# A spectral block's gradients on one core: c's gradient as a row, tables in two parts, one block placed elsewhere, more buffers at the end, another order

## The chip, the core and the metric

The kernel runs on one core of a Trainium2 chip. The core has five engines that run side by side, each with its own queue of instructions in a fixed order: PE (TensorE, matrix products; PEld is its loading of weights), DVE (VectorE), ACT (ScalarE), POOL (GpSimd) and SP (SyncE, which here does nothing but issue transfers). Sixteen DMA engines move data between DRAM and the on-chip memory SBUF; matrix products land in PSUM. Waits between engines go by semaphores. The metric is device time in microseconds (us) of one execution.

## What is computed

Forward and backward of one block, with x of 2048 rows by 512, in bfloat16. The reference is the vjp of this function, and returns its output and nine gradients:

```python
def _A_ref(x, w_r, w_i):                       # a filter in the 2-D Fourier domain
    X = rfft2(x) * (w_r + 1j * w_i)            # 2048 x 257 coefficients
    return irfft2(X, (S, D))
def _B_ref(x, w1, b1, w2, b2):                 # 512 -> 1792 -> 512
    r = relu(x @ w1 + b1); h = r * r
    return h @ w2 + b2
mod = (silu(c) @ w_mod)                        # six rows of 512: sa, ca, ga, sb, cb, gb
h = layernorm(x) * (1 + ca) + sa
x = x + ga * _A_ref(h, A_w_r, A_w_i)
h = layernorm(x) * (1 + cb) + sb
return x + gb * _B_ref(h, B_w1, B_b1, B_w2, B_b2)
```

The outputs are out_0 (the block's output) and the gradients of A_x (out_1), A_w_r and A_w_i (out_2, out_3), B_w1, B_b1, B_w2, B_b2 (out_4 to out_7), c (out_8, 512 values) and w_mod (out_9).

## The kernel before

The Fourier transforms are matrix products with tables of sines that are made on the chip. The rows' transform goes in two steps, with the table TA and with the tables LF; LF has 16 blocks of 128 by 128, each in three parts (first, second, and the first negated), so that real and imaginary parts come out of plain products. LG is LF transposed, for the way back. Cd and Cf are the tables of the columns' transform. The negated part lets a product read parts 0, 1 or 1, 2 as neighbours.

The work runs in stages:

- **Start (0 to about 50 us)**: loads, tables (`build_lf` makes LF on DVE and ACT), the modulation rows, the layer norm of 16 row tiles, and the first transform step (`spec_f1_half`). Between them PE makes products of grad_out with w2 transposed (`back_products`, L837), which nothing else waits for yet.
- **First spectrum (about 50 to 85 us)**: `spec_f23` makes the coefficients Xs in eight groups; `cmul` (L415 to L418, DVE) multiplies them with the filter Z; every second group Xs is stored to the scratch tensor xs_dram (L869). Beside it `lg_part` transposes a quarter of LF into LG by a DMA (L850) and stores it to LG_dram (L852); L826 stores LF to LF_dram. `spec_g1` (L352, L355) goes back with LG.
- **Four row blocks (about 85 to 265 us)**: `stage_g`, `stage_h` (L1009), `stage_o` and `stage_gn` (both L1038): the second layer norm, the dense part, its backward, and the transform of the gradient.
- **Second spectrum (about 265 to 330 us)**: `spec_f23` on the gradient, with LF reloaded in four pieces LFb (L1170, L1311), the filter Z and the stored Xs reloaded into two blocks Xb (L1314, buffers Xb_0 and Xb_1). `cmul` makes the filter's gradients in place in Xb, which L1332, L1337 and L1339 store to out_2 and out_3. Between its groups PE fills in `grad_w1` (L1281). LG comes back as LGb (L1346), and `spec_g1` uses it. L1359 loads grad_out again as g_sb in two halves, which `scale_g` (L1400) multiplies.
- **Last stage (about 330 us to the end)**: pairs of rows go through `spec_g2` (L372, its result Tsb is written by ACT at L374), `spec_g3` (L382), and `row_pair` and `row_end` (L1448 to L1468) to out_1. PE fills in the rest of `grad_w1` and then `grad_w2` (L1378), one of 14 blocks hn against g_sb at a time; hn is loaded from h_dram by a DMA transpose (L1201). `gm.emit` (L459 to L473) makes w_mod's gradient and sums for c, and L1498 to L1502 finish c's gradient.

At the very end c's gradient stands as gcb, 128 partitions by 4 values, and is stored with each value to its own place:

```python
with nc.allow_non_contiguous_dma(reason="512 values"):
    nc.sync.dma_start(out_8.rearrange("b (dc p) -> p (b dc)", p=P), gcb)
```

Memory is handed out by pools that are stacked, some from the left and some from the right (`Slots`). A tile in a pool that lies where a released pool was has to wait until the last reader of the old tile is done, a store among them. Before the change the stack on the left is, from below: gw1 and G (`gwa`), the LGb tables (`lg2`), Z (`spb`), then Xb and the products p (`f23b`, `ewb`); the buffers of the last stage (`fin2`, called fp) come from the right over the place of the upper ones.

The order of the instructions is written out by hand: `ORDER` has a list per engine. The numbers count that engine's instructions in the order in which the program makes them (SP: its 290 DMA issues); `set_order` ties each to the one before it in the list. So an SP issue that waits holds up all issues behind it.

Of the kernel before, what the change touches and what calls it, by code (L numbers as in the profile page):

```python
# [198 lines left out]
def build_lf(tc, K, cpool, g, sm, krs):  # L199
# [23 lines left out]
    LF = cpool.tile([P, 16, 3, P], BF16, name="LF")  # L223
    K["LF"] = [LF[:, 2 * gi:2 * gi + 2] for gi in range(8)]
    K["LFall"] = LF
    for q in range(4):
# [10 lines left out]
        for i in range(2):  # L237
            for x in range(2):
                V.tensor_tensor(LF[:, 4 * q + n0:4 * q + 4, i, 64 * x:64 * x + 64].rearrange("p n (a b) -> p n a b", b=4),
                                w[:, i, n0:4, 64 * x:64 * x + 64].rearrange("p n (a b) -> p n a b", b=4),  # L240
                                mk[:, x, None, None, :].broadcast_to([P, 4 - n0, 16, 4]), op=ALU.mult)
            for h in range(n0):
                V.tensor_tensor(LF[:, h, i, 0:64].rearrange("p (a b) -> p a b", b=4), w[:, i, h, 0:64].rearrange("p (a b) -> p a b", b=4),
                                mk[:, 2 + h, None, :].broadcast_to([P, 16, 4]), op=ALU.mult)
                V.tensor_tensor(LF[:, h, i, 64:128].rearrange("p (j a b) -> p j a b", j=2, b=2),
                                w[:, i, h, 64:128].rearrange("p (j a b) -> p j a b", j=2, b=2),
                                mk[:, 4, :].rearrange("p (j b) -> p j b", j=2)[:, :, None, :].broadcast_to([P, 2, 16, 2]), op=ALU.mult)
        nc.scalar.activation(LF[:, 4 * q:4 * q + 4, 2, :], LF[:, 4 * q:4 * q + 4, 0, :], AF.Copy, scale=-1.0)

# [56 lines left out]
def spec_f23(tc, K, UT, AEs, dc, dest, elementwise, after=lambda gi: None):  # L306

    nc = tc.nc
    with Slots(tc, name="psB", bufs=1, space=PSUM) as psB_pool, \
         Slots(tc, name="psC", bufs=2, space=PSUM) as psC_pool:  # L310
        def f3(gi):
            ae = AEs[gi % 2]
            tl = dest(gi)
            for hh in range(2):
                ps = psC_pool.tile([P, 2, 512], FP32, name="psC")
                for o in range(2):
                    for cs in range(2):
                        nc.tensor.matmul(ps[:, o, 0:DF], lhsT=K["LF"][gi][:, hh, o + cs, :], rhs=ae[:, hh, 256 * cs:256 * cs + DF],
                                         start=(cs == 0), stop=(cs == 1))
# [22 lines left out]
def spec_g1(tc, K, Z, CS, after=None):  # L342

    nc = tc.nc
    with Slots(tc, name="psG", bufs=6, space=PSUM) as psG_pool:
        for gi in range(8):
            for hh in range(2):
                n = 2 * gi + hh
                ps = psG_pool.tile([P, 2, 2 * P], FP32, name="psG")
                for y in range(2):  # L350
                    for ri in range(2):
                        nc.tensor.matmul(ps[:, 0, P * y:P * y + P], lhsT=Z[gi][:, hh, ri, 2 * y:255 + 2 * y:2],  # L352
                                         rhs=K["LG"][:, n, ri + y, :], start=(ri == 0), stop=(ri == 1))
                for ri in range(2):
                    nc.tensor.matmul(ps[:, 1, :], lhsT=Z[gi][:, hh, ri, 1:256:2],  # L355
                                     rhs=K["LG"][:, n, ri:ri + 2, :].rearrange("p y m -> p (y m)"), start=(ri == 0), stop=(ri == 1))
# [84 lines left out]
class GMod:  # L441
# [12 lines left out]
    def emit(self, jc, q, row, pool, ppool, nbuf=2, last=False):  # L454
# [24 lines left out]
        "0-17 106 18-21 135-142 22-27 143-146 28-29 147-154 30-31 155-158 32-35 159-166 36-37 167-170 38-45 175-178 171-174 50-51 "  # L479
        "183-186 179-182 52-53 86-89 46-47 187-190 48-49 191-194 90-93 195-202 58-61 54-57 203-206 94-97 66-69 211-214 98-101 "  # L480
        "62-65 207-210 102-105 70-71 107-110 74-75 72-73 76-77 219-222 215-218 78-85 111-126 223-226 303 127-134 304-311 227-234 "
        "312-321 235-242 328-330 243-246 322-323 331-334 324-325 335 326-327 251-254 336-337 340-343 338-339 247-250 344-359 "
        "255-258 360-366 372-373 367 374-375 368-369 259-262 370-371 376-383 388-389 263-266 390-391 384-385 448-451 386-387 "
        "452-455 460-463 456-459 267-270 464-470 476-477 471 478-479 472-475 271-274 484-487 480-483 279-282 275-278 512-513 "
        "488-489 514-517 287-290 490-491 500-501 283-286 518-519 492-493 506-507 494-495 502-503 496-497 504-505 508-509 498-499 "
        "510-511 548-549 520-521 524-525 550-551 526-527 522-523 528-529 536-537 530-535 538-539 542-543 540-541 544-545 552-555 "
        "546-547 560-563 566-569 556-559 564-565 578-579 572-573 570-571 580-581 574-577 582-583 291-294 585-588 295-298 589-593 "
        "299-302 594-598 392-395 608-611 607 396-399 612 653-656 400-403 666-669 665 404-407 679-682 678 408-411 692 412-415 693 "
        "691 416-419 599 420-423 600 694 601-603 695 604-606 424-427 849-852 428-435 696 862-864 436-439 865 613 440-443 614-620 "
        "444-447 861 883-885 584 621-624 641-644 625-632 886 633-640 645-652 657-664 670-677 683-690 697-808 896-897 809-824 898 "  # L490
        "825-832 841-848 853-860 899 866-869 833-840 874-881 870-873 882 887-895 901-914 900 1053 915-928 1054 929-942 1055-1056 "
        "943-956 1066 957-970 1067 971-1012 1068 1017-1020 1013-1016 1021-1024 1029-1032 1025-1028 1069 1065 1033-1036 1045-1052 "
        "1057-1064 1070-1073 1087-1090 1037-1044 1078-1085 1074-1077 1086 1091-1094 1100 1099 1101-1102 1095-1098 1103 1105-1118 "
        "1104 1119-1232 1253 1249 1233-1236 1250 1254-1255 1237-1248 1251 1257-1264 1252 1256 1269-1272 1265-1268 1281-1284 "
        "1305-1311 1285-1296 1301-1304 1297-1300 1273 1277-1278 1274 1327-1333 1279 1316-1322 1280 1338-1344 1323-1325 1275-1276 "
        "1349-1355 1312-1315 1326 1360-1366 1371-1377 1334 1382-1388 1345 1335 1346 1336 1347 1337 1348 1393-1406 1367-1370 "
        "1356-1359 1407-1420 1378-1379 1389-1390 1380 1391 1381 1392 1437-1450 1425-1427 1421 1428 1422-1424 1451-1464 1433 "
        "1429-1430 1434 1431 1435-1436 1432 1465-1488 1505-1520 1489-1491 1521 1497-1498 1492 1501-1502 1493 1503-1504 1494 "
        "1499-1500 1495-1496 1538-1553 1522-1524 1530-1531 1534-1535 1532-1533 1525-1528 1536-1537 1529 1554-1633 1643-1644 "
        "1635-1638 1647-1648 1645-1646 1639-1641 1649-1650 1642 1651-1666 1683 1691-1692 1695-1698 1634 1684-1689 1693-1694 "  # L500
        "1699-1714 1690 1667-1682 1744-1745 1732-1733 1731 1734-1735 1746-1747 1736-1738 1740-1743 1739 1715-1730 1764-1779 "
        "1748-1763 1781-1782 1793-1794 1789-1790 1795-1796 1780 1791-1792 1783-1788 1797-1812 1829-1830 1837-1838 1831-1832 "
        "1839-1844 1833-1836 1813-1828 1865-1866 1861-1862 1867-1868 1863-1864 1845-1860 1891-1892 1909-1910 1885-1886 1915-1916 "
        "1887-1888 1893-1894 1917-1918 1911-1912 1895-1896 1919-1920 1903-1906 1897-1902 1913-1914 1889-1890 1907-1908 1869-1884 "
        "1927-1930 1951-1954 1921-1922 1933-1934 1931-1932 1939-1940 1923-1926 1941-1942 1945-1946 1943-1944 1935-1938 1947-1948 "
        "1963-1966 1957-1958 1967-1968 1955-1956 1975-1976 1959-1960 1969-1970 1961-1962 1977-1978 1971-1972 1979-1980 1973-1974 "
        "1949-1950 1989-2004 1981-1988 2005 2007-2012 2006 2013-2030 2053 2048 2054 2049 2055 2050 2056 2051-2052 2047 2031-2046 "
        "2079 2083 2073 2084 2080-2081 2074 2082 2085-2086 2057-2072 2129 2125 2130 2119 2126-2127 2209-2224 2075-2078 2121-2124 "
        "2128 2131-2132 2087-2102 2155 2120 2156 2103-2118 2133-2148 2159-2160 2150 2161-2162 2157-2158 2149 2163-2178 2201-2202 "
        "2205-2208 2203 2196 2204 2179-2194 2151-2154 2197-2200 2243-2246 2309-2310 2195 2225-2240 2251 2247 2252-2254 2248 2242 "  # L510
        "2249-2250 2255-2270 2241 2277-2292 2272 2271 2293-2308 2311-2326 2273-2276 2327-2416"
    ),
    "ACT": (
        "0-1 3 2 8 7 4-6 13 10 16 50 11 51 17 12 9 52-53 20 14 54 15 55 18-19 56 23-24 57 37-38 58 27 21-22 42 59-60 30 26 25 31 "
        "39 29 34 40 28 62 61 44 32 41 33 63 45 35 43 36 46 64 79 47 65 80 66 48 67 81-83 68 84-86 88 87 69 89 91 90 92 49 94 93 "
        "104 106 105 70 107 109 108 77 71 110-111 73 72 78 112-114 74 115-119 121 75 122-124 128 76 132 131 95 133 147 96 151 150 "
        "158 125 154 97 126 98 127 161 99 162 129 100 134 187 130 135 101 136 102 191 163 137 103 138 120 139-146 148-149 152-153 "
        "159-160 155 164 157 156 166 198 167 165 168-170 173 171-172 174 179 176 180-181 175 182-183 178 184-186 177 188-190 192 "
        "202 194 193 199 201 200 203 195 197 196 227 204-210 212 211 213-214 220 215 219 216 221-223 218 224-226 217 231 228-229 "
        "238 230 232 234 233 239-243 235 237 236 244 247 245-246 248-250 252 251 254 253 259-260 255 261-262 256 264 263 267-268 "  # L520
# [1028 lines left out]
```

## Time and profile before

| | us |
|---|---|
| three runs: median (lowest to highest) | 424.77 (424.04 to 427.11) |
| the profiled execution, whole | 424.7 |
| its span | 422.9 |
| PE busy in the span | 382.3 (2417 matmuls) |
| DVE, ACT busy | 342.7, 276.7 |
| DMA | 93.59 MB, 221 GB/s on average |
| last matmul ends | 405.65 |
| mean granted clock of TensorE | 0.974 of full |

The profile is of one execution. Its times count from the start of the span. A row of the timeline has start, duration, engine, line, operation, the tile written and the tiles read, and in brackets the idle time before it and what ended it. A row of the waits has who waited, for what, and in total, how often and the longest. A row by stretches has the stretch, its length, the busy time of PE, PEld, DVE, ACT and POOL (with the count of instructions), the granted clock as a share, the mean busy share of the DMA engines, and GB/s. In the page's second part the span is cut in 40 equal slices, and each digit is a busy share in tenths. "To landing" is the time from a DMA's issue until its semaphore says that it has landed.

### The profile page before, as it was taken

Reading aid. Unit: us, or ns where it says so; the run is one execution under the profiler, and the core shown is the slowest. Engines: PE = TensorE matmul, PEld = TensorE weight load, DVE = VectorE, ACT = ScalarE, POOL = GpSimd, SP = SyncE. Lnnn points to the kernel's source line nnn. Section 1 sums busy time; section 2 is a strip of 40 time slices with the busy share of each in tenths; the row PEclk is TensorE's granted clock in tenths of the full one; section 3 lists DMA queues with packets and bytes.
Section 4 is the critical chain, followed back from the end, with each engine's and each line's share of the span. In section 5 each row is a group of like instructions: output and inputs, shape, how many; then the busy total and the mean of one; then the engine's idle time right before and its main releaser. Section 6 shows DMA issues by size and latency. Waiting matters only on the chain.

```text
span 422.9 us, 6929 instructions
## 1 busy us (share of the span) xinstructions
PE 382.3 (90%) x2417; PEld 201.3 (48%) x2417; DVE 342.7 (81%) x826; ACT 276.7 (65%) x493; POOL 14.4 (3%) x56
## 2 busy tenths in 40 slices
PE   0799999989999999999999999999999499999930
PEld 0355565745444444444444454655567354444430
DVE  6899879956996999799999999289999177877930
ACT  4569999779733793487168584676564378678920
POOL 5322000000000000000000000000000000000000
PEclk9999999999999999999999999999999799999975
DMA  8999999998855595669659989899899999999750
GB/s 256 212 251 285 288 208 255 298 201 239 285 110 173 146 244 133 133 182 222 173 130 233 244 222 262 241 351 342 236 324 213 228 187 255 267 242 233 195 155 0
DMA packets 144212, 93.59 MB, mean 221 GB/s; under 512 B 98347, under 2 KB 130097, under 8 KB 143665
## 3 DMA queue, kind: packets, MB, share of 16 engines
q1 hardware_dynamic: 143468, 92.55, 87.0%
q10 hardware_dynamic: 708, 0.59, 0.6%
q8 instruction: 19, 0.31, 0.3%
q14 instruction: 17, 0.13, 0.1%
HBM read 37.39 MB, written 34.24 MB: 169 GB/s over the span
## 4 chain that ended last, share of the span: by engine, by line
PE 62%; DVE 11%; DMA 9%; SPq 8%; ACT 4%; issue 2%; ACTq 0%; DVEq 0%
PE og_0s L1038 9%; PE og_1s L1038 9%; PE mm_0s L1281 5%; PE mm_1s L1378 5%; PE mm_1s L1009 4%; PE mm_0s L1009 4%; PE mm_1s L837 3%; PE mm_1s L1281 3%; PE mm_0s L1378 3%; PE mm_0s L837 3%; PE pst L1009 3%; DMA xs_dram<-Xs_3s 2%; SPq L692 2%; SPq L689 2%; DMA g_sb<-in_grad_out_dram 2%
## 5 line engine op out<-in xcount | busy, mean ns | idle before, releaser
L1281 PEld LDWEIGHTS <-h_sb 128*128 128x128 bf16 x256 | 25.0, 99 | 22.5 <-issue 1.8
L1038 PEld LDWEIGHTS <-gab 128*128 128x128 bf16 x224 | 21.6, 98 | 25.5 <-DVE gab L1016 0.7
L1009 PEld LDWEIGHTS <-w 128*128 128x128 bf16 x224 | 21.2, 98 | 25.1 <-issue 1.9
L837 PEld LDWEIGHTS <-w2T 128*128 128x128 bf16 x224 | 21.4, 99 | 21.7 <-DMA w2T<-in_B_w_dram 2.9
L1281 PE MATMUL mm_0s<-gab,h_sb 128*128 128x384 bf16 (+1 forms) x160 | 30.2, 342 | 0.0
L1038 PE MATMUL og_0s<-w1T,gab 128*128 128x512 bf16 x112 | 26.0, 379 | 0.0
L1038 PE MATMUL og_1s<-w1T,gab 128*128 128x512 bf16 x112 | 25.7, 379 | 0.0
L336 ACT ACTIVATE AE<-psB 128x1024 bf16<-128x1024 f32 x16 | 22.0, 1375 | 1.6 <-PE psB L332 1.4
L1281 PE MATMUL mm_1s<-gab,h_sb 128*128 128x512 bf16 (+1 forms) x96 | 21.9, 384 | 0.0
L1009 PE MATMUL mm_1s<-h2T,w 128*128 128x512 bf16 x84 | 21.6, 379 | 0.0
L1009 PE MATMUL mm_0s<-h2T,w 128*128 128x512 bf16 x80 | 20.5, 379 | 0.0
L1378 PE MATMUL mm_1s<-g_sb,hn_0s 128*128 128x512 bf16 x80 | 18.1, 379 | 1.3 <-ACT gw_0s L1379 1.0
L1378 PE MATMUL mm_0s<-g_sb,hn_1s 128*128 128x512 bf16 (+1 forms) x80 | 16.4, 358 | 0.0
L837 PE MATMUL mm_1s<-gT_0s,w2T 128*128 128x512 bf16 x56 | 14.4, 379 | 1.9 <-DMA w2T<-in_B_w_dram 1.9
L837 PE MATMUL mm_0s<-gT_0s,w2T 128*128 128x512 bf16 x56 | 15.2, 395 | 0.5 <-DMA w2T<-in_B_w_dram 0.5
L372 PEld LDWEIGHTS <-utcs 128*128 128x128 bf16 x128 | 10.6, 100 | 10.3 <-issue 3.8
L1009 PE MATMUL pst<-h2T,w 128*128 128x512 bf16 x60 | 15.4, 379 | 0.0
L837 PE MATMUL mm_0s<-gT_1s,w2T 128*128 128x512 bf16 x56 | 14.4, 379 | 0.0
L837 PE MATMUL mm_1s<-gT_1s,w2T 128*128 128x512 bf16 x56 | 14.4, 378 | 0.0
L841 ACT CAST gab<-mm_1s 128x512 bf16<-128x512 f32 x20 | 12.0, 601 | 3.1 <-PE mm_1s L837 3.0
L1378 PEld LDWEIGHTS <-hn_1s 128*128 128x128 bf16 x96 | 9.3, 98 | 7.6
L1378 PEld LDWEIGHTS <-hn_0s 128*128 128x128 bf16 x80 | 7.7, 97 | 10.6 <-issue 1.9
(622 smaller groups left out, 1031.2 us busy)
## 6 DMA issues: line engine op xcount, KB each, us to landing
w<-in_B_w_dram SPq DMA_DIRECT2D x2, 1792.0 KB
Z<-wz_dram SPq DMA_DIRECT2D x4, 514.0 KB, 5.3
x_sb<-in_A_x_dram SPq DMA_DIRECT2D x2, 1024.0 KB, 7.3
n_dram<-x_sb SPq DMA_DIRECT2D x4, 512.0 KB, 3.2
h_dram<-h2r SPq DMA_DIRECT2D x8, 256.0 KB, 2.3
h_sb<-h_dram SPq DMA_DIRECT2D x4, 512.0 KB
g_sb<-in_grad_out_dram SPq DMA_DIRECT2D x2, 1024.0 KB
LF_dram<-LF SPq DMA_DIRECT2D x4, 384.0 KB, 5.8
```

The costliest lines, as they stand in the source:

```text
L336: nc.scalar.activation(dst, ps.rearrange("p r (s e f) -> p (r s) e f", s=2, e=2), AF.Copy, scale=EF_S)
L372: nc.tensor.matmul(ps[:, P * i:P * i + P], lhsT=CS[:, t, i].rearrange("p a b -> p (a b)"), rhs=K["Cf"][:, i, :], start=True, stop=True)
L689: q.dma_start(w2T[:, :, a:z], B_w2[a:z, :], transpose=True)
L692: q.dma_start(gT[b].rearrange("p j c q -> p (j c) q"), g_view[:, TB * b:TB * b + TB, :].rearrange("p j d -> p (j d)"), transpose=True)
L837: nc.tensor.matmul(ps, lhsT=w2T[:, dc, fc * P:(fc + 1) * P], rhs=gT[b][:, :, dc, :], start=(dc == 0), stop=(dc == 3))
L841: nc.scalar.copy(out=gaT[b][:, fc, :], in_=ps)
L1009: nc.tensor.matmul(ps, lhsT=w1[:, dc, (fc + i) * P:(fc + i + 1) * P], rhs=h2T[b][:, :, dc, :], start=(dc == 0), stop=(dc == 3))
L1038: nc.tensor.matmul(ps, lhsT=lhs(fc), rhs=rhs[:, fc, :], start=(fc == 0), stop=(fc == NFC - 1))
L1281: nc.tensor.matmul(blocks(ps, fb), lhsT=h2_sb[:, t, dc * P:(dc + 1) * P], rhs=gh_rows(t, fb), start=(t == 0), stop=(t == NT - 1))
L1378: nc.tensor.matmul(ps[:, 0:w], lhsT=hns[fc][:, t, :], rhs=g_sb[:, t, c:c + w], start=(t == 0), stop=(t == NT - 1))
```

## The change

c's gradient gcb is transposed on PE into PSUM (4 rows of 128), copied to SBUF by DVE, and stored as four rows of 256 bytes.

The tables LF and LG are laid out anew: by quarters, then by part, then by block. Their scratch tensors LF_dram and LG_dram hold two parts instead of three; stores, transposes and reloads move two parts, and the third is made on the chip: LG's by DVE behind each transpose, LFb's and LGb's by ACT behind each reload.

Of the two blocks Xb the second gets a pool of its own, `frb`, below the tables in the stack; it is released after the load of rows 4.

The pool at the end (`endp`) has six hn buffers instead of four, and once it exists also eight gw buffers, gh1 and q1 (three each) and gs (six); before that these have two each. hn is loaded up to ten blocks ahead instead of eight.

All five lists of `ORDER` are new.

```diff
-    LF = cpool.tile([P, 16, 3, P], BF16, name="LF")
-    K["LF"] = [LF[:, 2 * gi:2 * gi + 2] for gi in range(8)]
+    LF = cpool.tile([P, 4, 3, 4, P], BF16, name="LF")
+    K["LF"] = [LF[:, gi // 2, :, 2 * (gi % 2):2 * (gi % 2) + 2] for gi in range(8)]
...
-                                     rhs=K["LG"][:, n, ri:ri + 2, :].rearrange("p y m -> p (y m)"), start=(ri == 0), stop=(ri == 1))
+                    nc.tensor.matmul(ps[:, 1, :].rearrange("p (y m) -> p y m", y=2), lhsT=Z[gi][:, hh, ri, 1:256:2],
+                                     rhs=K["LG"][:, n // 4, ri:ri + 2, n % 4, :], start=(ri == 0), stop=(ri == 1))
...
-        "2249-2250 2255-2270 2241 2277-2292 2272 2271 2293-2308 2311-2326 2273-2276 2327-2416"
+        "2225-2240 2271 2255-2270 2272 2277-2308 2273-2276 2327-2334 2309-2326 2351 2335-2350 2368 2352-2367 2369-2417"
...
-        "2 4 0-1 7 3 18 5 8 10 22 6 9 11 30 26 15 21 29 19 116 16 49 12 20 14 17 87 27 23 31 91 28 79 34 25 35 43 24 41 13 38 37 "
+        "2 4 0-1 7 10 3 5-6 8 118 23 9 29 19 11 28 30 14 16 12 20 15 17 26 21 49 31 116 25 32 38 22 18 27 24 41 122 79 13 35 46 "
...
-        "200 208 215 217 201 225 214 209 219 193 220 202 223 221 232 227-228 230 229 231 222 226 235 213 234 224 233 236 247 253 "
-        "266 246 238 267 245 242 240 252 239 251 243-244 258 254 249-250 248 237 264 269 262 256 255 241 272 263 259-260 274 257 "
-        "268 261 276-277 271 273 279 275 281 265 280 278 282 284 270 283 285 287 286 289 288"
+        "216 211 181 179 199 203 213 225 218 201 220 198 219 212 182 184 214 224 222 221 229 236 227 237 228 226 233 232 231 230 "
+        "241 234 247 235 246 253 267-268 239 251-252 260 245 243 255 240 242 272 244 249 274 264 256 258 257 269 262 276 259 250 "
+        "254 263 271 275 238 261 279 277-278 270 265-266 248 283 282 284 280 285 287 281 286 288 273 289"
...
-    LF_dram = dram.tile([4, P, 4, 3, P], BF16, name="LF_dram")
-    LG_dram = dram.tile([4, P, 4, 3, P], BF16, name="LG_dram")
+    LF_dram = dram.tile([4, P, 2, 4, P], BF16, name="LF_dram")
+    LG_dram = dram.tile([4, P, 2, 4, P], BF16, name="LG_dram")
...
     def lg_part(q):
-        nc.sync.dma_start(K["LG"][:, 4 * q:4 * q + 4].rearrange("p a y m -> p (a y) m"),
-                          K["LFall"][:, 4 * q:4 * q + 4].rearrange("p a y m -> p (a y m)"), transpose=True)
-        nc.sync.dma_start(LG_dram[q], K["LG"][:, 4 * q:4 * q + 4])
+        nc.sync.dma_start(K["LG"][:, q, 0:2].rearrange("p y a m -> p (y a) m"), K["LFall"][:, q, 0:2].rearrange("p y a m -> p (y a m)"), transpose=True)
+        nc.vector.tensor_scalar(K["LG"][:, q, 2], K["LG"][:, q, 0], -1.0, None, op0=ALU.mult)
+        nc.sync.dma_start(LG_dram[q], K["LG"][:, q, 0:2])
...
-                    nc.sync.dma_start(LF1[g], LF_dram[g])
+                    nc.sync.dma_start(LF1[g][:, 0:2], LF_dram[g])
+                    nc.scalar.activation(LF1[g][:, 2], LF1[g][:, 0], AF.Copy, scale=-1.0)
...
-            hns.append(pool.tile([P, NT, P], BF16, name="hn", bufs=2 if pool is not endp.get("hn") else 4))
+            hns.append(pool.tile([P, NT, P], BF16, name="hn", bufs=2 if pool is not endp.get("hn") else 6))
...
     gwa = Slots(tc, name="gwa", bufs=1)
+    frb = Slots(tc, name="frb", bufs=1)
     lg2 = Slots(tc, name="lg2", bufs=1)
...
-                nc.sync.dma_start(LF2[g - 2], LF_dram[g])
+                nc.sync.dma_start(LF2[g - 2][:, 0:2], LF_dram[g])
+                nc.scalar.activation(LF2[g - 2][:, 2], LF2[g - 2][:, 0], AF.Copy, scale=-1.0)
...
-                Xt[0] = fr.tile([P, 2, 2, 4, FP], BF16, name="Xb", bufs=2)
+                Xt[0] = (frb if g else fr).tile([P, 2, 2, 4, FP], BF16, name="Xb", bufs=1)
...
-                    nc.sync.dma_start(K["LG"][:, 4 * k:4 * k + 4], LG_dram[k])
+                    nc.sync.dma_start(K["LG"][:, k, 0:2], LG_dram[k])
+                    nc.scalar.activation(K["LG"][:, k, 2], K["LG"][:, k, 0], AF.Copy, scale=-1.0)
...
-            last = fc == NFC - 1
-            gwh[fc] = (endp["gm"] if last else gwp).tile([P, D], BF16, name="gw", bufs=1 if last else 3)
+            late_ = "gm" in endp
+            gwh[fc] = (endp["gm"] if late_ else gwp).tile([P, D], BF16, name="gw", bufs=8 if late_ else 2)
...
-        while len(hns) < min(NFC, max(fc + 4, min(2 * fc + 6, 8))):
+        while len(hns) < min(NFC, max(fc + 4, min(2 * fc + 6, 10))):
...
     load_rows3(4)
+    frb.release()
...
-            gh1 = fp.tile([P, 2, D], BF16, name="gh1", bufs=3)
-            q1 = fp.tile([P, 2, D], BF16, name="q1", bufs=3)
+            gh1, q1 = [(endp["gm"].tile([P, 2, D], BF16, name=x, bufs=3) if "gm" in endp else fp.tile([P, 2, D], BF16, name=x, bufs=2)) for x in ("gh1", "q1")]
             gn = fp.tile([P, 2, D], BF16, name="gn")
-            gs = fp.tile([P, 2, D], BF16, name="gs", bufs=3)
+            gs = (endp["gm"].tile([P, 2, D], BF16, name="gs", bufs=6) if "gm" in endp else fp.tile([P, 2, D], BF16, name="gs", bufs=2))
...
-        with nc.allow_non_contiguous_dma(reason="512 values"):
-            nc.sync.dma_start(out_8.rearrange("b (dc p) -> p (b dc)", p=P), gcb)
+        pg = psX.tile([4, P], BF16, name="mm")
+        nc.tensor.transpose(pg, gcb, K["ident"])
+        gcr = fp.tile([4, P], BF16, name="gcr", bufs=1)
+        nc.vector.tensor_copy(gcr, pg)
+        nc.sync.dma_start(out_8.rearrange("b (dc p) -> (b dc) p", p=P), gcr)
```

## The prediction

> **What bounds the kernel now.** I read four views in this order: the page's first two parts, the waits, the timeline around the two longest gaps, and busy time by stretches. The first shows that TensorE sets the pace, and that the last fortieth of the span has nothing on any engine.
>
> ```profile
> PE 382.3 (90%) x2417; PEld 201.3 (48%) x2417; DVE 342.7 (81%) x826; ACT 276.7 (65%) x493; POOL 14.4 (3%) x56
> PE   0799999989999999999999999999999499999930
> DMA  8999999998855595669659989899899999999750
> ```
>
> By stretches, PE is busy 36.5 of 37 us (25 to 62), 42.6 of 45 (62 to 107), 124.0 of 124 (107 to 231), 33.6 of 34, 40.0 of 40 (265 to 305), 35.0 of 35 (337 to 372) and 31.2 of 33 (372 to 405). So removing work from DVE or ACT is worth little; what counts is where PE stands idle: 12.9 us in the first 25, 5.3 between 330 and 336, about 5 in scattered pieces, and everything after its last matmul at 405.65. The waits and the timeline name the two long ones.
>
> ```profile
> SPq L1544 <- DMA out_dram<-gcb_0s: 15.4, 1, 15.4
> ...
> ACT Tsb_0s L374 <- DMA out_dram<-Xb_1s: 5.6, 1, 5.6
> ...
> PE psY_0s L382 <- DMA g_sb<-in_grad_out_dram: 5.3, 1, 5.3
> ...
> SPq L1273 <- DMA out_dram<-Xb_1s: 6.9, 3, 5.5
> ```
>
> ```profile
> 405.25 0.37 SPq L1502 DMA_DIRECT2D out_dram<-gcb_0s  x1
> 405.68 0.37 ACT L1379 CAST gw<-mm_0s 128x256 bf16<-128x256 f32 x1 [1.17 <-PE mm_0s L1378]
> 405.71 0.50 SPq L1380 DMA_DIRECT2D out_dram<-gw  x1
> 406.09 0.39 ACTq L1380 DMA_DIRECT2D out_dram<-gw  x1
> ```
>
> L1502 stores c's gradient, 512 values of 2 bytes to 512 separate addresses. SP then waits 15.4 us (406.2 to 421.6); the span ends 1.3 us later. The DMA view of 404 to 423 (40 slices of 0.48 us) shows that the bytes have gone by 408, so the wait is for the stores to be acknowledged, not for a backlog:
>
> ```profile
> DMA  9999749100004000000000000000000000000000
> GB/s 336 354 310 353 124 63 216 0 0 0 0 0 1 0 0 0 0 0 0 0 0 0 0 0 0 0 0 0 0 0 0 0 0 0 0 0 0 0 0 0
> ```
>
> In the other gap the wait named for PE (g_sb) is only the last event; PE waited for ACT's Tsb (335.08), whose buffer lies on the spectrum block Xb_1 and had to wait until Xb_1's stores had landed.
>
> ```profile
> 330.00:335.00 5.00, 0.38 (x7) 0.21 (x4) 0.00 (x0) 0.00 (x0) 0.00 (x0) 0.78 1.08 251
> 335.00:340.00 5.00, 4.27 (x17) 2.19 (x18) 1.44 (x4) 3.53 (x7) 0.00 (x0) 0.54 0.94 205
> ```
>
> All engines are empty, and the granted clock falls to 0.54: the next sixteen matmuls (L1281, mm_1s) take 4.72 us where an undisturbed group takes 3.62.
>
> **The change, part by part**, against the profiled execution: 424.7 us, span 422.9 and 1.8 around it. The median of the runs is 424.77, so nothing has to be shifted.
>
> *c's gradient as a row.* It removes the 15.4 us wait. It adds, after the last matmul (405.65; the new transpose is last in PE's list): a transpose of 128x4, between 0.1 (a weight load) and 0.4 (L459's 0.38), taken 0.3; a DVE copy of 4x128, 0.16 (gcb) to 0.68 (L360, 128x512), taken 0.2; two hand-overs, 0.3 together; the issue, 0.4. Landing isn't shown for a row of 256 bytes: rows give 2.0 (gw_1s, 128 KB), 4.4 (gwm_1s) and 9.1 (gwm_3s, in flight with the scattered store). I take 2.3, near gw_1s, as the backlog is gone by 408. With 1.3 to finish: 405.65 + 0.3 + 0.2 + 0.3 + 0.4 + 2.3 + 1.3 = 410.45, so **-12.4**. The last gw store, issued to 406.48, is landed by then. With a landing of 4.4 it is -10.3; with 0.8, as the bytes of the gw issued to 406.48 have gone by 407.3, -13.9.
> The row against a rule: the Trainium skill, "DMA: Bandwidth & Descriptors", section "Anatomy of one DMA", has a fixed cost of about 2.0 us per DMA whatever its shape, mostly the write receipt, and its "Specifications" count every run under 512 bytes as read-modify-write, which the 256-byte rows still are. By that the tail would gain nothing and the sum would be 417.9; the trace has 15.4 us, and no run here yet shows a row store.
>
> *Spectrum block below the tables.* Xb_1 goes under the LG tables, so the buffers of the last stage (Tsb, n, gh1) no longer lie on it. ACT's wait at L374 and SP's at L1273 lose their cause. PE's gap is 330.38 to 335.73, 5.3, and the clock costs 1.1 on the group and 0.3 on the short matmuls: 6.7. Next late would be the second half of g_sb: it lands at 335.75 and needs two DVE multiplications of 1.22, so 338.2; without the gap PE reaches grad_w2(0) at 346.30 - 6.7 = 339.6, and needs that half eight matmuls later, 341.3. The new SP list issues both g_sb loads ahead of Xb_1's stores, so it comes sooner. I take **-6.0**; the bounds are -6.7 and, if DMA holds the stage (below), -3.1.
>
> *Tables in two parts.* Twenty moves (LF and LG to DRAM, LG's transposes, LFb and LGb back) shrink from 384 to 256 KB: 2.6 MB less, 11.6 us of DMA time at the mean 221 GB/s; SP issues as many as before (290 in both lists). Added on ACT are eight negations of 128x512 at 0.72 (L468): two between 231 and 280, six between 290 and 318, where ACT is busy 25.7 of 40 us (265 to 305) and 15.6 of 32 (305 to 337). They hide there; were that cover gone, 5.8. Each waits for its load, and behind it in ACT's queue stand the evictions of psC (L320) and of psB (L336), for which PE's next L318 waits; the new SP list issues the LGb loads from place 180 on (before: 195), ahead of the negations by several evictions. On DVE four at 0.35 (L470), each waiting for its transpose (4.1 us to landing) with the products of L415 to L418 behind it. Three come before the last product of the first spectrum, where DVE is full (19.6 of 20 us, 60 to 80): +1.05 on its chain. Against that, 1.5 MB fewer between 46 and 88 at 250 GB/s frees 6 us of DMA, of which the last xs_dram store (10.15 us to landing, on the chain) profits; PE is idle only 2.4 us in 62 to 107. Between +1.05 and -2.4 I take **-0.5**. The strided table operand costs nothing: L1281 reads four strided rows at 379 ns per 512 columns, L1009 one contiguous row at 379.
>
> *More end buffers and the new order.* Eight gw, six hn and six gs buffers take away the waits on stores behind ACT's copies; PE idles 1.8 in 372 to 405. The order moves hundreds of places, but PE's list keeps its course; two places differ. At the start three w2T transposes are issued in one go behind an additional 512 KB load, where PE idles 3.3 (10 to 25). In the last stage a block of grad_w1 stands ahead of the first psY, which covers ACT's Tsb. The trace can't show the order: at best it recovers the idle of 10 to 25, 62 to 107 and 372 to 405, -7.5; at worst it makes one more gap like the one at 330, +5.3. I take **-0.3**.
>
> Sum: 424.7 - 12.4 - 6.0 - 0.5 - 0.3 = **405.5**.
>
> **The rivals.**
> - *DMA holds the last stage* (0.22). The DMA share is 0.9 to 1.3 in nearly every 5 us from 305 to 400, so PE could start earlier and wait later, for an hn. Then only bytes count: 768 KB of LFb and LGb at 247 GB/s, 3.1. 424.7 - 12.4 - 3.1 - 0.8 = 408.4, or 410.8 with a new gap of 5.3 on the forecast. Against it: no hn wait shows in PE's rows, and shares up to 1.4 occur (195 to 200), so 1.0 isn't full.
> - *The order also recovers the idle at the start and in the middle* (0.13): half of 7.5, 401 to 402, less with a short tail.
> - *The tail stays* (0.04): the 15.4 us is how any last store to DRAM ends. Then 417.9. Against it: gw_1s lands in 2.0.
> - *Slower, by SP's queue in the last stage* (0.03). The new list puts a store of grad_w1 that waits for PE's block [2031-2046] (about 337.5) ahead of hn 3 to 13; behind it, to hn 13, stand 11 transposes and 25 other issues (0.45 each, 11.3 us). PE ends at least 5.5 (landing) + 3.8 (two half blocks) after hn 13 is issued, the span 4.8 later. Slower by 1% needs hn 13 issued at 413.1: (413.1 - 337.5 - 11.3)/11 = 5.85 us of SP per transpose. The rows of L1201 have 2.3 to 4.4; L692 and L689 at the start have 6.95 and 6.50. From 5.85 on it is slower, about 430; a price of 4.4 to 5.85 gives about no change (0.03).
>
> **Chances and range.** The forecast's own case has 0.55, at 402 to 408. Low: forecast with the short tail (-1.5) and half the order's idle back (-3.7), about 400. High: 410.8 with the long tail (+2.1), 412.9. The range is 399 to 413; outside are the last two rivals, the no-change case and the ends of the others, under 0.2. Faster by over 1% (below 420.5; about what a measurement of this kernel can tell): 0.55 + 0.22 + 0.13 + 0.04 = 0.94; within 1% 0.03; slower 0.03.
>
> **What would show it.** Right: SP's closing wait under 3 us; span end less than 6 us after the last matmul; no wait of Tsb or of an n load for Xb_1; granted clock near 1.0 throughout 325 to 345; PE's last matmul at 398 to 400. Wrong: PE idle before L1378 with a DMA of hn or g_sb as its end (the DMA rival); SP rows of L1201 near 6 us; a negation (AF.Copy into LFb or LGb) with a long wait in front of an eviction; more than 13 us of idle PE before 25 us, which would be the order's.

## The result, and the profile after

The changed kernel takes **408.45 us** (median of 4 runs, 408.32 to 408.92) where the kernel before takes 425.31 (median of 4, 424.04 to 427.11): a ratio of **0.960**, 95% interval 0.957 to 0.964. The forecast was 405.5 with a range of 399 to 413. So the side, the size and the range hold, and the forecast is 3 us too fast. The profiled execution takes 408.54, with a span of 406.8.

First the page of the changed kernel, its first two parts (busy time; busy tenths in 40 slices):

```profile
PE 382.3 (94%) x2394; PEld 200.9 (49%) x2418; DVE 341.8 (84%) x831; ACT 278.4 (68%) x501; POOL 14.1 (3%) x56
PE   0998999999999999999999999899999997899996
PEclk9999999999999999999999999999999999899999
DMA  9999999487594789789877889969999999999997
```

PE's busy time reads the same as before, though 24 of the changed kernel's 2418 matmuls have no record in this profile (PEld has them all). Its last slice is a 6 and no longer a 0, so the empty tail has gone. The 4 at slice 32 has gone too, but there is a new dip (7, 8) at slices 34 and 35, and the clock's 8 beside it.

The end of the span, from the timeline of the changed kernel (start, duration, engine, operation):

```profile
401.32 1.91 PE L1382 MATMUL mm_0s<-g_sb,hn_3s 128*128 128x256 bf16 x16
...
403.16 0.22 PE L1506 MATMUL mm<-ident,gcb_0s 128*4 128x128 bf16 x1
...
403.42 0.21 DVE L1508 COPY gcr<-mm 4x128 bf16<-4x128 bf16 x1 [1.76 <-PE mm L1506]
403.67 0.37 ACTq L1384 DMA_DIRECT2D out_dram<-gw_5s  x1
403.75 0.30 SPq L1509 DMA_DIRECT2D out_dram<-gcr  x1
```

and SP's last wait, from the view of SP's waits (in total, times, longest):

```profile
SPq L1551 <- DMA out_dram<-gw_0s: 1.6, 1, 1.6
```

The transpose ends at 403.38 and the span at 406.8, so 3.4 us lie behind PE's end where there were 17.3 (405.65 to 422.9). That is 13.9 us less. SP's closing wait is 1.6 instead of 15.4, and it is for a store of grad_w2, not for c's gradient.

The old gap and what came in its place, by stretches of 5 us (PE, PEld, DVE, ACT, POOL busy; granted clock; DMA share; GB/s):

```profile
330.00:335.00 5.00, 5.00 (x36) 2.78 (x34) 3.48 (x3) 1.95 (x4) 0.00 (x0) 1.00 0.82 254
335.00:340.00 5.00, 4.95 (x39) 3.02 (x37) 3.46 (x8) 3.62 (x7) 0.00 (x0) 1.00 0.84 173
340.00:345.00 5.00, 2.81 (x15) 1.28 (x14) 1.18 (x3) 1.30 (x3) 0.00 (x0) 1.00 1.13 140
345.00:350.00 5.00, 3.11 (x14) 1.46 (x15) 0.76 (x2) 3.80 (x8) 0.00 (x0) 0.79 1.00 202
350.00:355.00 5.00, 5.00 (x30) 2.25 (x28) 3.56 (x11) 2.55 (x6) 0.00 (x0) 0.87 1.06 244
```

From 330 to 340 all is as forecast: PE full, clock 1.00. From 340 to 350 PE loses 4.1 us, and the clock falls to 0.79. The waits and the timeline name the cause:

```profile
ACT gs_0s L1452 <- DMA out_dram<-gw_1s: 4.4, 1, 4.4
...
PE psY_0s L382 <- ACT gs_0s L1452: 4.0, 1, 4.0
```

```profile
339.96 0.55 SPq L1290 DMA_DIRECT2D out_dram<-gw_1s  x1
340.56 7.97 SPq L1202 DMA_TRANSPOSE hn_1s<-h_dram  x2
...
346.20 0.58 ACT L1452 CAST gs_0s<-psY_0s 128x512 bf16<-128x512 f32 x1 [4.39 <-DMA out_dram<-gw_1s]
```

ACT's first write into the new pool endp has to wait until the last block of grad_w1, issued at 339.96, has landed (6.1 us). PE needs psY_0s evicted, so it stands too. This is the same kind of gap as the old one, 12 us later.

Where the 16.2 us between the two profiles come from, by PE's idle time before its last matmul (before, after; summed from busy time in the same stretches): 0 to 25: 12.9, 11.2. 25 to 62: 0.5, 1.5. 62 to 107: 2.4, 0.8. 107 to 305: 0.4, 2.3. 305 to 372: 5.4, 5.1. From 372 to PE's end: 1.8, 0.2. Together 23.3 and 21.1, so 2.2 of the 16.2 come from before PE's end, and 13.9 from the tail. From 305 to 372, where the forecast had 6.0, PE's idle time is 0.3 less. As records are missing, the share of each stretch is good to 1 or 2 us only: a second profile of the same kernel (the control below), which has all 2418, gives 10.8, 0.0, 0.7, 1.7, 4.5 and 0.1, together 17.8, with PE's end at 403.0 instead of 403.4.

### The profile page after: what moved, and what is told of

Its sections match the earlier page's. It is cut to its first block, busy times and chain, and to the rows that moved or that the text cites. A ratio compares the mean times of both kernels' runs of the same rounds, so it can differ in the third digit from the quotient of the medians.

```text
span 406.8 us, 6919 instructions
## 1 busy us (share of the span) xinstructions
PE 382.3 (94%) x2394; PEld 200.9 (49%) x2418; DVE 341.8 (84%) x831; ACT 278.4 (68%) x501; POOL 14.1 (3%) x56
## 5 line engine op out<-in xcount | busy, mean ns | idle before, releaser
L1283 PE MATMUL mm_1s<-gab,h_sb 128*128 128x512 bf16 (+1 forms) x96 | 20.8, 370 | 0.0
L372 PEld LDWEIGHTS <-utcs 128*128 128x128 bf16 x128 | 10.3, 97 | 13.0 <-issue 6.7
L837 PE MATMUL mm_1s<-gT_0s,w2T 128*128 128x512 bf16 x56 | 15.5, 394 | 0.7 <-DMA w2T<-in_B_w_dram 0.6
L1382 PE MATMUL mm_0s<-g_sb,hn_1s 128*128 128x512 bf16 x62 | 15.9, 412 | 0.1
L1009 PE MATMUL pst<-h2T,w 128*128 128x512 bf16 x60 | 15.4, 379 | 0.0
L841 ACT CAST gab<-mm_1s 128x512 bf16<-128x512 f32 x20 | 12.4, 622 | 4.0 <-PE mm_1s L837 3.9
L1382 PE MATMUL mm_1s<-g_sb,hn_0s 128*128 128x512 bf16 (+1 forms) x63 | 12.7, 352 | 0.1
L332 PEld LDWEIGHTS <-utcs 128*128 128x128 bf16 x128 | 9.3, 97 | 4.9 <-issue 1.8
L839 DVE CAST gab<-mm_0s 128x512 bf16<-128x512 f32 x12 | 8.2, 686 | 3.5 <-PE mm_0s L837 3.5
```

Of the source, the lines that this page charges most:

```text
L332: nc.tensor.matmul(ps[:, hh, P * co:P * co + P], lhsT=UT[:, c, 2 * gi + hh, :, :], rhs=K["Cd"][:, P * c:P * c + P], start=not extra, stop= ...
L372: nc.tensor.matmul(ps[:, P * i:P * i + P], lhsT=CS[:, t, i].rearrange("p a b -> p (a b)"), rhs=K["Cf"][:, i, :], start=True, stop=True)
L837: nc.tensor.matmul(ps, lhsT=w2T[:, dc, fc * P:(fc + 1) * P], rhs=gT[b][:, :, dc, :], start=(dc == 0), stop=(dc == 3))
L839: nc.vector.tensor_copy(out=gaT[b][:, fc, :], in_=ps)
L841: nc.scalar.copy(out=gaT[b][:, fc, :], in_=ps)
L1009: nc.tensor.matmul(ps, lhsT=w1[:, dc, (fc + i) * P:(fc + i + 1) * P], rhs=h2T[b][:, :, dc, :], start=(dc == 0), stop=(dc == 3))
```

## The experiments

In each, one thing is changed in the changed kernel; line numbers move by up to five, and the numbers in an engine's order are places in the order in which its instructions are written. The runs stand in three groups, each with runs of the kernel before on the same chip. That took 428.48 us (f_split, c_scatter, x_old2, t_three), 424.19 (after_ctl, f_split2, c_128x8, c_half) and 428.05 (m_pool, t_three2, c_line, c_spread), with single runs from 423 to 432. So medians and ratios to it are both given, and differences under 2 us are left open. The changed kernel itself ran again in the second group only. For the first, an estimate: c_scatter's 421.75 less its longer tail of 12.6 (the table below) puts the changed kernel on that chip at 409.1.

### The changed kernel itself

The same kernel, once more, beside two of the experiments below.

> The changed kernel itself, beside the runs of this call, since the kernel before takes 428.5 on the chip of the last call and 425.3 on that of the result: every theory 0.9603 of the kernel before, to be subtracted from.

Measured: 408.18 (406.64 to 411.13), ratio 0.962 (0.959 to 0.966). Below, "the changed kernel" is 408.2 to 408.5, or 0.960 to 0.962.

### The store of c's gradient: undone, then taken apart

```
c_scatter:
-        pg = psX.tile([4, P], BF16, name="mm")
-        nc.tensor.transpose(pg, gcb, K["ident"])
-        ...
-        nc.sync.dma_start(out_8.rearrange("b (dc p) -> (b dc) p", p=P), gcr)
+            nc.sync.dma_start(out_8.rearrange("b (dc p) -> p (b dc)", p=P), gcb)
```

> The changed kernel with only the store of c's gradient as before: 512 values of 2 bytes to 512 addresses, no transpose, no copy. Theory A (the acknowledgement of these small writes is the tail): SP's closing wait is about 15 us again and the median 408.45 + 13.7 = 422.2 (421 to 423). Rival B (the tail of before came from the many stores in flight at its end, which the new order spreads): under 412, with a closing wait under 6 us.

Measured: **421.75** (420.99 to 422.69), ratio 0.985 (0.979 to 0.991). That is 13.3 above the changed kernel by the medians, about 10 by the ratio, and 12.6 by the ends of the two profiles (the table below). PE ends at 403.3 here and at 403.4 in the changed kernel, so all of it lies behind PE. SP's closing waits in this run:

```profile
SPq L1552 <- DMA out_dram<-gw_0s: 8.8, 1, 8.8
SPq L1552 <- DMA out_dram<-gcb_0s: 5.3, 1, 5.3
```

Together 14.1. The tail is this store and nothing else. The first of the two lines is worth a look: an ordinary store of 128 KB, issued 0.5 us earlier on the same queue, is acknowledged only 8.8 us into the wait. The next four runs ask what about the store is slow; c_128x8 stores the values in another order, and the other three leave half or most of them out.

```
c_128x8:  out_8.rearrange("b (p dc) -> p (b dc)", p=P), gcb             128 pieces of 8 bytes
c_half:   out_8.rearrange("b (dc p) -> p (b dc)", p=P)[:, 0:2], gcb[:, 0:2]     256 of 2 bytes
c_line:   out_8.rearrange("b (dc p) -> p (b dc)", p=P)[0:32, 0:1], gcb[0:32, 0:1]  32 neighbours
c_spread: out_8.rearrange("b (j q) -> j (b q)", q=16)[:, 0:1], gcb[0:32, 0:1]   32, 32 bytes apart
```

> The run c_scatter with the same 512 values stored as 128 pieces of 8 bytes (each partition's four values side by side, so c's gradient comes out in another order than the reference's). If the wait at the end goes with the number of pieces: 15.4 x 128/512 = 3.9 us in place of about 14, and a span of 408 to 410. If any store of tiny pieces is acknowledged that late, whatever their number: span 419. If pieces of 8 bytes are like rows: 406.8.

> The run c_scatter with only the first 256 of the 512 values stored, 2 bytes each to an address of its own; the other half of c's gradient is left out. If the wait goes with the number of pieces: half of c_scatter's 14.1, about 7, span 412 to 413. If it is the same for any such store: span 419.

> The run c_scatter with only 32 of the 512 values stored, 2 bytes each, to 32 neighbouring addresses, 64 bytes in all; the rest of c's gradient is left out. If the late acknowledgement comes from pieces that fall into the same few bytes and are written one after the other (256 and 512 pieces of 2 bytes had 32 to every 64 bytes and took as long; 128 pieces of 8 bytes had 8 and took a quarter): about 14 us again, span 419. If it goes with the number of pieces, or of pieces to 512 bytes (32 of 256): 2 us or less, span 407.

> The run c_scatter with 32 of the 512 values stored, 2 bytes each, at addresses 32 bytes apart, the rest of c's gradient left out. If the wait comes from pieces in the same 64 bytes (two here): 1 to 2 us, span 407. If it is a property of pieces of 2 bytes: 14 us, span 419.

Measured, one profile each, from the start of the last issue (c's gradient) to the end of the span, which leaves out that PE itself ends up to 2 us earlier or later from run to run:

| run | pieces | in the same 512 bytes | issue to end, us | above the row |
|---|---|---|---|---|
| the row (changed kernel) | 4 of 256 B | 2 | 3.0 | |
| c_spread | 32 of 2 B | 16 | 3.2 | 0.2 |
| c_line | 32 of 2 B | 32 | 4.8 | 1.8 |
| c_128x8 | 128 of 8 B | 64 | 5.5 | 2.5 |
| c_scatter | 512 of 2 B | 256 | 15.6 | 12.6 |
| before | 512 of 2 B | 256 | 17.7 | 14.7 |
| c_half | 256 of 2 B | 256 | 17.8 | 14.8 |

In the row and in c_spread SP's closing wait is for an ordinary store (gw_0s), so 3.0 and 3.2 only bound what their own store takes, and the row's value is 2.6 in the control: those two can't be told apart. Half the pieces cost no less, so it doesn't go with their number: here the expectation of 412 to 413 falls. It is not a property of 2-byte pieces either, as c_spread shows, nor of pieces that share 64 bytes, as c_line had 32 of them there and no 14 us. What orders the table is how many pieces fall into the same 512 bytes: about 0.04 to 0.06 us for each from 32 on, the two blocks of 512 side by side. That 512 is the right size and not merely one that fits is not shown: counted by 256 bytes, with 8, 32, 32 and 128 pieces from c_spread to c_half, the table keeps its order too. Each run has one profile, and the three with 256 pieces differ by up to 2.2 us. The bytes themselves leave at once, as the DMA view of c_half, 400 to 420 in 40 slices of 0.5 us, shows:

```profile
DMA  9999985000000000000000000000000000000000
```

with SP's closing waits of the same run:

```profile
SPq L1552 <- DMA out_dram<-gcb_0s: 13.5, 1, 13.5
SPq L1552 <- DMA out_dram<-gw_5s: 1.8, 1, 1.8
SPq L1552 <- DMA out_dram<-gw_0s: 1.0, 1, 1.0
```

The DMA engines are idle from 403.5 on, 1.2 us after the issue has ended, and the span ends at 419.8. Here the ordinary store gw_0s is acknowledged 1.0 us into the wait, so the 8.8 of c_scatter is not the rule. The Trainium skill, "DMA: Bandwidth & Descriptors", "Specifications", has runs below 512 bytes as read-modify-write. No run shows how such pieces are written. What the runs show is a price only where many of them meet in the same 512 bytes: the row's runs of 256 bytes are below 512 too, and end in 3.0 us from issue to the end of the span.

### The new gap: cut the pool

```
f_split:
                     endp["hn"] = endp["gm"] = Slots(tc, name="endp", bufs=2)
+                    endp["top"] = Slots(tc, name="endq", bufs=2)
-                gm.load(0, endp["gm"])
-                gm.load(1, endp["gm"])
+                gm.load(0, endp["top"])
+                gm.load(1, endp["top"])
```

(the column sums acc1_odd and acc1_sb go with it). The buffer gs_0s keeps its place, bytes 29,056 to 31,104 of each partition, over the old buffer gab; grad_w1's buffers lie at 86,432 to 93,888. In the changed kernel's program the copy into gs_0s waits on seven DMA semaphores, in f_split's on none. In the kernel before, endp ended at byte 64,896, over the old gab alone (24,960 to 84,352); the added end buffers take it to 104,832, over grad_w1's. So it is the end buffers' edit that made the new wait, not the move of the spectrum block.

> The pool endp is cut in two at the place where the old gab pool ended; every buffer that the last stage touches first (gs, gh1, q1, gw, hn) keeps its address, the two late ones (the modulation weights and the column sums) go into a second pool above. Theory A (the new gap at 342 to 346 is a wait for the store of grad_w1's last block, which ACT's first write into endp takes over because the pool as a whole lies over that block's buffers, though this buffer doesn't): PE's 4.0 us before psY_0s L382 and the clock's 0.5 to 0.8 after it go, median 403.5 to 404.5 against 408.45 for the changed kernel. Rival B (DMA holds the stage, as the DMA share of 1.13 between 340 and 345 could say): PE gets to its next hn earlier and waits there, 407 to 408.5, with PE idle before L1382 and an hn as its end.

Measured: 407.43 (405.71 to 409.90), ratio 0.952 (0.947 to 0.958); span 405.7 against 406.8. The gap at 342 is gone; the same stretch in f_split:

```profile
340.00:345.00 5.00, 4.95 (x30) 2.53 (x30) 1.55 (x5) 4.56 (x10) 0.00 (x0) 1.00 1.14 109
```

So the cause is shown: the pool's first user waited for **everything** that lay under the pool, whatever its own address. What that is worth is less clear: the median is 1 us lower, as rival B has it, the ratio 3.5 to 4 us lower, as theory A has it, and against the estimate of 409.1 for this chip it is 1.7. Part of the idle time moved on, as PE's waits of f_split show:

```profile
PE mm_0s L1382 <- DMA hn_5s<-h_dram: 2.7, 1, 2.7
PE acc L1440 <- DVE q_0s L1458: 1.6, 2, 1.0
```

Then the late load was brought forward, one entry of SP's list:

```
f_split2, SP's order:   "... 255 240 242 272 244 249 274 264 256 ..."  ->  "... 255 256 240 242 272 244 249 274 264 ..."
```

> The cut pool of the run f_split, and one place of SP's list: the load of hn for the tenth block of grad_w2 (hn_5s, whose buffer is free) goes from behind the loads for the eleventh and twelfth, which wait for buffers that PE still reads, to ahead of them. Theory A (after the cut it is the order of SP's queue that makes PE wait 2.7 us for hn_5s): the wait goes, and the median is 3.5 to 4.5 below the changed kernel's in this call. Rival B (DMA holds the stage: whatever is loaded earlier makes something else later): within 1.5 of it, as f_split's profile is (span 405.7 against 406.8), with another load as the end of PE's waits.

Measured: 407.31 (405.53 to 408.93), ratio 0.959 (0.956 to 0.962), against the changed kernel's 408.18 on the same chip: no difference that can be told, again rival B. The wait for hn_5s has gone, and another has come. PE's longest new wait in f_split2, and two rows of its timeline:

```profile
PE mm_1s L1386 <- ACT gw_6s L1387: 2.4, 1, 2.4
```

```profile
373.76 0.69 DVE L1476 TENSOR_TENSOR gs_2s<-gs_2s,gxl_0s 128x1024 bf16<-128x1024 bf16 x1 [4.07 <-DMA gxl_0s<-gx_dram]
...
374.44 0.59 ACT L1457 CAST gs_0s<-psY_0s 128x512 bf16<-128x512 f32 x1 [2.74 <-DMA out_dram<-gs_0s]
```

Both waits are for transfers that now stand behind hn_5s on SP: the row load gxl_0s is issued at 369.15 and the store of gs_0s at 369.77, in f_split at 366.16 and 366.77. ACT, held by the store and then by DVE's lateness, copies gw_6s at 377.55, in f_split at 373.41, and PE waits for it. Last, 17 plain stores were moved from SP to POOL:

```
m_pool:
-            nc.sync.dma_start(out1_view[:, t:t + 2, :], gx)
+            nc.gpsimd.dma_start(out1_view[:, t:t + 2, :], gx)
(and the same for grad_w2's stores of blocks 0 to 8)
```

> The cut pool of f_split, and 17 plain stores of the last stage (nine of grad_w2's, all eight of the second gradient's rows) issued from POOL, which is idle there, in place of SP; about 17 x 0.45 = 7.6 us less of SP's time between 342 and 400, the same bytes. Theory A (SP's queue, which issues back to back from 338 on, holds the last stage): PE's 4.6 us of idle time between 372 and 400 shrink to under 2, 3 us or more below the changed kernel, 0.952 of the kernel before or less. Rival B (the DMA engines hold it): the transposes on SP take as much longer as the stores freed, and the time stays within 1.5 of the changed kernel, 0.957 to 0.963.

Measured: 407.46 (405.85 to 411.83), ratio 0.954 (0.949 to 0.959): between the two expectations by the ratio, with B by the median, and the same as f_split (407.43, 0.952) either way. Its profile is of the slowest of its six runs (411.83), so its stretches are a rough guide. PE's idle time from 372 to 400 is 3.0 where f_split has 4.6, not the under 2 of theory A. SP's plain issues between 330 and 396 take 13.1 us (24) where f_split has 17.7 (38). Its twelve transposes take 44.9, in f_split 43.0, in f_split2 41.2 and in the changed kernel 38.7, so that they take longer because the stores are gone, as rival B has it, can't be told from this spread.

After each of the three repairs another wait stands in front of PE, and the three medians lie between 407.3 and 407.5: about 1 us below the changed kernel by the medians, 1 to 4 by the ratios. That fits a last stage held by its transfers taken together, but doesn't prove it. The DMA share there is 0.95 to 1.1. Whether it is the engines, or SP's transposes (2.0 to 5.2 us each in the changed kernel), stays open, since m_pool still has SP busy for 58 of 66 us.

### The spectrum block: back in its old place

```
x_old2:
-    frb = Slots(tc, name="frb", bufs=1)
-                Xt[0] = (frb if g else fr).tile([P, 2, 2, 4, FP], BF16, name="Xb", bufs=1)
+                Xt[0] = fr.tile([P, 2, 2, 4, FP], BF16, name="Xb", bufs=2)
SP's order: "229 236 227 237 228 226 233 232 231 230" -> "229 227 228 232 231 230 236 237 226 233"
```

> The changed kernel with both spectrum blocks in one pool as before, above the tables, and ten places of SP's list changed so that it can run: the six stores of the second block go ahead of the load of row pair 4, two stores of grad_w1 and one hn. By the term of the prediction (6.0) a gap of about 5 us at 330 comes back, with its clock: 413.5 to 414.5. Rival (the gap was replaced by the one at 342, both wait for stores on the same queue, so only one of the two can show in full): 409.5 to 411, with the gap at 330 back and the one at 342 gone.

Measured: 412.00 (410.92 to 413.51), ratio 0.963 (0.957 to 0.969): 3.6 slower by the medians, 2.9 against the estimate of 409.1 for this chip, hardly slower by the ratio; its profile has the span 3.1 longer (409.9). In its waits the old gap is back:

```profile
ACT Tsb_0s L374 <- DMA out_dram<-Xb_1s: 9.7, 1, 9.7
PE psT_1s L372 <- ACT Tsb_1s L374: 6.8, 1, 6.8
```

and ACT's copy into gs_0s waits 0.3 us instead of 4.4. The time lies between the two expectations, the mechanism is the rival's: the gaps replace each other, and undoing the edit costs about 3 (less by the ratio), not 6. What SP's changed list costs alone wasn't run.

### The tables: three parts again

```
t_three:
-    LF_dram = dram.tile([4, P, 2, 4, P], BF16, name="LF_dram")
+    LF_dram = dram.tile([4, P, 3, 4, P], BF16, name="LF_dram")
-                nc.sync.dma_start(LF2[g - 2][:, 0:2], LF_dram[g])
-                nc.scalar.activation(LF2[g - 2][:, 2], LF2[g - 2][:, 0], AF.Copy, scale=-1.0)
+                nc.sync.dma_start(LF2[g - 2], LF_dram[g])
(and so for LG, the first LFb and the transposes; the negations leave ACT's and DVE's lists)
```

> The changed kernel with the tables carried in three parts: 384 KB instead of 256 KB in each of the twenty moves, no negation on ACT (eight fewer) or DVE (four fewer), all else in the same order. By the prediction's term 0.5 slower, bounds 1.05 faster to 2.4 slower: 407.4 to 410.9. Rival (DMA held the stages between 46 and 88 and from 290 on): 3 or more slower, over 411.4.

Measured: 418.07 (416.28 to 419.07), ratio 0.976 (0.971 to 0.981): 9.6 slower by the medians, 6 to 7 by the ratio, 7.7 by the spans: on the rival's side, and far beyond the forecast's term. PE stands for 8.3 us at about 85 to 94. Before that, in the timeline of t_three ACT's late negations of LF (L248)

```profile
64.19 0.76 ACT L248 ACTIVATE LF<-LF 128x512 bf16<-128x512 bf16 x1
70.03 0.74 ACT L248 ACTIVATE LF<-LF 128x512 bf16<-128x512 bf16 x1
```

are followed at once by SP's store and transpose of that part of the table:

```profile
64.98 0.36 SPq L830 DMA_DIRECT2D LF_dram<-LF  x1
70.79 1.45 SPq L854 DMA_TRANSPOSE LG<-LF  x1
...
84.83 0.48 SPq L872 DMA_DIRECT2D xs_dram<-Xs_2s  x1
...
92.88 0.34 SPq L918 DMA_DIRECT2D x_0s<-in_A_x_dram  x1
```

Each SP instruction starts as the negation before it ends, and all that stands behind them on SP is late, down to the store of Xs_2s: 84.83, in the changed kernel 78.51. ACT's Tsb_0s and SP's load x_0s, which both start at 92.9 (in the changed kernel at 85.64 and 85.31), wait for the stores at the end of this row, and PE for Tsb_0s, as the waits of t_three show:

```profile
SPq L918 <- DMA xs_dram<-Xs_2s: 6.7, 1, 6.7
ACT Tsb_0s L374 <- DMA LF_dram<-LF: 9.0, 1, 9.0
PE psY L382 <- ACT Tsb_0s L374: 8.3, 1, 8.3
```

With two parts SP needs only the parts that DVE makes (LF's first store is issued at 60.45), and ACT's negations, in the changed kernel at 65.25 and 71.10, hold up nobody on SP. To tell this from the bytes, the two late negations were moved forward:

```
t_three2, ACT's order: the negation of LF's third quarter 11 places, of the fourth 16 places earlier
```

> The run t_three (tables carried in three parts) with two of ACT's four negations L248, of the third and fourth quarter of LF, moved 11 and 16 places forward in ACT's list (from about 65 and 71 us to about 58 and 61). Theory A (t_three lost its time because SP's stores and transposes of three parts wait for these negations, and with two parts they don't): PE's gap of 8.3 us at L382 goes, and the time is 0.962 to 0.968 of the kernel before (408 to 410.5 where that takes 424.2). Rival B (the extra 2.6 MB): it stays near t_three's 0.976, with the gap.

Measured: 413.51 (411.48 to 414.16), ratio 0.966 (0.963 to 0.970); PE's wait at L382 falls from 8.3 to 0.9. Of the 9.6 us some 4.6 were this dependency in this order (the two runs are on chips where the kernel before takes 428.48 and 428.05). The rest (5.1 by the medians, 2 to 2.5 by the ratio) holds the bytes and what the moved negations cost where they now stand: ACT waits 2.0 us for DVE's table before one of them, and PE's idle time between 25 and 62 is 3.3 in place of 1.5 (0.0 in the control).

## Why the prediction was right, and where it was wrong

**c's gradient (-12.4): right, and 1.5 too small.** 13.9 in the profiles, 10 to 13 by undoing it. Of the sum 405.65 + 0.3 + 0.2 + 0.3 + 0.4 + 2.3 + 1.3 the oversized terms are the last two: from the end of the issue (404.05) to the end of the span it is 2.7, not 3.6. The sum of 417.9, by which the tail would have gained nothing, is not what the runs show. Nor does it follow from the fixed cost of 2.0 us that the prediction takes from the Trainium skill: in place of the landing of 2.3 that gives an estimate of 410.15. The skill fits that figure to transfers that GpSimd issues; the row's store is issued by SP.

**Spectrum block (-6.0): the step that failed.** The old wait went as forecast, clock included. "Next late would be the second half of g_sb" was wrong: next late was gs_0s, behind the last store of grad_w1, in the very pool that the change enlarges. So the gain was lost to a wait that another of the edits made: the prediction took the end buffers only as removing waits on stores. The profiles show 0.3 less idle time in that stretch, undoing the edit about 3. The prediction also gave the old wait a wrong reason. Tsb's own bytes (Tsb_0s at 100,096 to 101,120) do not lie on Xb_1 (130,912 to 139,136); the pool around it, 96,000 to 129,920, lies over that of the spectrum blocks. With the right reason the new endp, which now takes ACT's first writes, would have had to be looked at in the same way. The case was in the text only as "one more gap like the one at 330, +5.3", the worst end of the order's term.

**Tables (-0.5) and order (-0.3): small in sum, as forecast, but not by the reasons given.** PE's idle time outside the gap's stretch falls by 1.9 us in all: 1.7 less from 0 to 25, 1.6 less from 62 to 107 and 1.6 less from 372 on, with 2.9 given back between 25 and 62 and between 107 and 305. In the control, with no record missing, only 0.8 is given back there, and PE ends 0.4 earlier; how the gain is shared isn't firm. The negations are hidden; none stands in front of an eviction for long. What the sum left out is that three parts tie SP's queue to ACT's negations; in the new order that alone is worth more than the whole term. So the terms of these two edits can't be told apart by taking one back.

**The sum.** The parts gave -13.9, -0.3 and about -2.0 where the forecast had -12.4, -6.0 and -0.8. The failed term is 5.7 too large; that the whole is only 3 us off is luck, since the others gave 2.7 more than forecast.

**The rivals.** The DMA rival (408.4) gave the measured time almost to the digit, but by chance: in the changed kernel the wait is the pool's, and no hn ends PE's idle time. Its mechanism may stand behind that wait: after f_split the last stage waits for one transfer or another, whatever is moved. The tail stayed short, SP's transposes stayed between 2.0 and 5.2 us (from 5.85 on it would have been slower), and the start got 1.7 better.

**The signs.** SP's closing wait under 3 us: 1.6. Span end less than 6 us after the last matmul: 3.4. No wait of Tsb or of an n load for Xb_1: right (DVE's multiplication of g_sb has 1.7 us put down to such a store, and PE doesn't wait for it). Clock 1.00 from 325 to 345: right, and 0.79 after it. PE's last matmul at 398 to 400: wrong, 403.2, and these 4 us are the new gap and its clock.

## What to carry to other kernels

When a pool of buffers is moved off a late store, ask which instruction is now the first to touch *any* pool whose region holds a late store: here it waited for all that lay there, and cutting the pool at the right place removed the wait without moving that buffer. Enlarging a pool asks the same question. A gap in front of a stage that is full of transfers can be worth less than its length: removing it twice here, by 5.3 and by 4.0 us, gave about 3 and 1 by the medians, and by the ratios under 1 and about 4. Undoing one edit under an order made for all of them prices the order too, so look for the dependency that the edit removed, here SP's on ACT's negations, before calling the difference the edit's cost.

## What the runs showed of the hardware that was not expected

In these runs a last store of 2-byte pieces ended 13 to 15 us later than the row when 256 of them fell into the same 512 bytes, though the DMA engines were idle 1.2 us after its issue (c_half); 256 or 512 pieces in all made no difference, and 32 pieces spread 32 bytes apart cost 0.2, which is within the spread. Ordinary stores near it were late in two of three such runs: gw_0s, issued just before on the same queue, was acknowledged 8.8 us into the wait in c_scatter, and in the kernel before the next store, 64 KB, took 16.1 us to landing; in c_half it was 1.0.
